# Attention with a block mask, then a gated feed-forward: the first batch loaded by casting transfers, transposed two token tiles at a time, and masked by rows copied on chip

## The chip, the cores and the metric

One core of a Trainium2 chip. The metric is the device time of one execution in microseconds (us), median over several executions.

Engines are named as the profile names them: PE is TensorE (PEld its weight loads), DVE VectorE, ACT ScalarE, POOL GpSimd, SP SyncE. Each engine works through its own instructions in the order in which the program lists them.

## The reference, cut to what matters

```python
# q, k, v: (4 batches, 8 heads, 768 tokens, 64), float32
scores = scale * q @ k.T                    # per batch and head
scores = where(mask, scores, -1e9)          # mask: blocks of 32 x 32 tokens,
                                            # window, first/last block, 3 sampled blocks per row
attn   = softmax(scores)
x      = (attn @ v)                         # as (3072 tokens, 512)
xn     = x / sqrt(mean(x*x) + 1e-6) * rms_g
out    = (silu(xn @ w_gate) * (xn @ w_val)) @ w_out     # 512 -> 1536 -> 512
```

The kernel adds the mask inside the scores matmul: besides the 64 rows of a head, K and Q carry 24 more, one for each block of 32 tokens. K has a 1 in the row of its block, and Q has 0 or -32768 in each row.

## The kernel before: the parts that matter here

Heads are worked in pairs, four to a batch. A unit is a strip of one to three query tiles of 128 tokens, over all eight heads; when the four pairs of a unit have been through attention, its rows can be normalised and go through the feed-forward. Until then PE has no feed-forward work.

```python
KQ = D + NB                                                   # 64 + 24 = 88
UNITS = [(0, 0, 1), (0, 1, 1), (0, 2, 2), (0, 4, 2)]          # (batch, first tile, tiles)
...
# mask columns go into the buffer aug, beside K and Q, before the transposes
nc.vector.tensor_copy(out=aug[0][:, 0, :, :, D:KQ], in_=kmb)
nc.scalar.copy(out=aug[0][:, 1, :, :, D:KQ], in_=qmb)
...
def fill(g, i, eng):              # cast a float32 load to bfloat16, into aug
    copy(eng, aug[g % NAUG][:, i, :, :, 0:D], raws[g][:, i]...)
...
def tp(g, i, n, pool):            # one transpose for each head and token tile, mask columns with it
    ...
        nc.tensor.transpose(
            out=t_[0:KQ, m, :], in_=aug[g % NAUG][:, i, e, c, 0:KQ], identity=ident)
```

Everything after a hand-written start is put in order by a list scheduler at build time. It takes, again and again, the instruction that can start first by its own table of durations, from start times that are also given by hand:

```python
free = {"PE": 5.2, "ACT": 6.0, "DVE": 4.9, "POOL": 4.9, "DMA": 2.1}
...
kk = (int(t1 * 20), o["prio"], o["n"])      # earliest start, then priority
```

The order is fixed when the kernel is built; what differs on the chip only makes engines wait.

The softmax here doesn't subtract the row's maximum and nothing guards it: scores larger than these inputs give would overflow.

## Time and profile before

| | before |
|---|---|
| time, median of the first 3 runs (range) | 313.67 us (313.28 to 314.38) |
| span of the profiled run | 311.3 us |
| first transpose of K | 6.07 us |
| first scores | 8.04 us |
| first gate matmul of the feed-forward | 28.56 us |
| first output matmul | 45.59 us |

The last four rows are starts in the timeline of PE. They mark how far the kernel is: attention can begin, attention runs, the first unit has been through all four pairs, the feed-forward's first product is ready. The page, windows and chain of this kernel are shown in the prediction. Two more views are needed to read what follows. The first is the head of VectorE in the timeline (start, length, engine, line, operation, tiles):

```profile
4.68 0.24 DVE L139 TENSOR_SCALAR Bneg<-Bm 32x32 bf16<-32x32 bf16 x1
...
5.28 0.73 DVE L190 CAST aug<-qkv 128x768 bf16<-128x768 f32 x1
```

The mask is ready by 5 us, and the next work is the cast of the first pair. The second is PE in the same view:

```profile
6.07 0.98 PE L220 MATMUL tp<-ident,aug 128*88 128x128 bf16 x14 [0.80 <-DVE aug L190]
...
8.04 0.50 PE L243 MATMUL s__202<-X 88*128 88x128 bf16 x6
...
28.56 1.06 PE L346 MATMUL gp<-xn,wg 128*128 128x128 bf16 x16
```

### The profile page before, as it was taken

The page shows a single profiled execution, that of the slowest core. Times are in us where ns is not written, and L with a number is a line of the kernel's source. Part 1 is how long each engine was busy: PE and PEld are TensorE (multiplying, and loading weights), DVE is VectorE, ACT ScalarE, POOL GpSimd, SP SyncE. Part 2 cuts the span into 40 slices and gives each one's busy share as a digit, 9 for nine tenths or more (in the row PEclk, how much of TensorE's full clock was granted, in tenths as well). Part 3 has the DMA queues.
Part 4 walks back from the last instruction along what each step waited for, and adds up shares of the span by engine and source line. Part 5 has one row for each costly group of instructions (what it writes and reads, how often), then busy time and mean ns, then how long its engine had stood idle before and what let it go on. Part 6 is the DMA issues. An engine that isn't in the chain of part 4 may idle for free.

```text
span 311.3 us, 7229 instructions
## 1 busy us (share of the span) xinstructions
PE 300.7 (97%) x3015; PEld 201.8 (65%) x3015; DVE 188.0 (60%) x411; ACT 204.1 (66%) x306; POOL 26.3 (8%) x44
## 2 busy tenths in 40 slices
PE   6899999998999999999999999999999999999994
PEld 3888998776777766665666666666656556546541
DVE  6775487756468859646755844754587627517600
ACT  3789888788778778787887877877623333233312
POOL 5594000000001001001000100100010000000000
PEclk9999999999999999999999999999999999999999
DMA  7999996999999999710972300030012020020022
GB/s 222 393 196 203 243 285 137 259 334 220 250 357 254 228 262 273 158 37 2 186 161 45 84 2 35 2 86 6 31 47 40 2 99 3 0 101 2 0 101 101
DMA packets 69187, 42.39 MB, mean 136 GB/s; under 512 B 48036, under 2 KB 65956, under 8 KB 69156
## 3 DMA queue, kind: packets, MB, share of 16 engines
q1 hardware_dynamic: 63328, 37.23, 45.7%
q0 software_dynamic: 5792, 4.72, 9.8%
q8 instruction: 23, 0.38, 0.5%
q14 instruction: 8, 0.07, 0.1%
q10 hardware_dynamic: 36, 0.00, 0.0%
HBM read 28.57 MB, written 6.29 MB: 112 GB/s over the span
## 4 chain that ended last, share of the span: by engine, by line
PE 90%; DMA 5%; ACT 2%; DVE 1%; SPq 0%; issue 0%; POOL 0%; ACTq 0%; DVEq 0%
PE gp L346 20%; PE yp L379 20%; PE vp L346 20%; DMA X<-aug 2%; DMA qkv<-in_k_dram 2%; ACT pt L254 2%; PE tp L220 1%; PE tr L314 0%; SPq L70 0%; PE o__3524 L268 0%; PE o__2246 L268 0%; PE o__2882 L268 0%; PE o__1425 L268 0%; PE o__3944 L268 0%; PE o__3095 L268 0%; PE o__2679 L268 0%
## 5 line engine op out<-in xcount | busy, mean ns | idle before, releaser
L361 DVE SCALAR_TENSOR_TENSOR uu<-th,gp 128x384 bf16<-128x384 bf16 (+1 forms) x90 | 52.1, 580 | 69.0 <-ACT th L355 67.3
L346 PE MATMUL gp<-xn,wg 128*128 128x384 bf16 (+2 forms) x480 | 74.3, 294 | 0.8 <-DVE uu L361 0.8
L346 PE MATMUL vp<-xn,wv 128*128 128x384 bf16 (+2 forms) x480 | 74.3, 294 | 0.0
L379 PE MATMUL yp<-wo,hp 128*128 128x512 bf16 x288 | 69.7, 379 | 0.0
L355 ACT ACTIVATE th<-gp 128x384 bf16<-128x384 f32 (+1 forms) x90 | 46.3, 514 | 33.5 <-PE gp L346 31.5
L346 PEld LDWEIGHTS <-wg 128*128 128x128 bf16 x480 | 43.2, 98 | 22.6 <-issue 1.0
L370 DVE TENSOR_TENSOR hp<-uu,vp 128x384 bf16<-128x384 bf16 (+1 forms) x90 | 50.3, 577 | 12.0 <-PE vp L346 11.2
L346 PEld LDWEIGHTS <-wv 128*128 128x128 bf16 x480 | 43.1, 97 | 21.2
L243 PEld LDWEIGHTS <-X 88*128 88x128 bf16 x480 | 40.8, 97 | 20.1 <-issue 2.2
L379 PEld LDWEIGHTS <-hp 128*128 128x128 bf16 x288 | 28.1, 98 | 28.4
L268 PEld LDWEIGHTS <-pt 128*128 128x128 bf16 x1152 | 41.5, 97 | 5.8 <-ACT pt L254 1.7
L388 ACT ACTIVATE yo<-yp 128x512 f32<-128x512 f32 x23 | 13.8, 598 | 29.9 <-PE yp L379 29.6
L297 POOL TENSOR_TENSOR rs<-ms,nhalf 128x3 f32<-128x3 f32 (+2 forms) x10 | 7.8, 777 | 195.0 <-DVE ms L290 195.0
L190 DVE CAST aug<-qkv 128x768 bf16<-128x768 f32 x28 | 15.3, 560 | 4.8 <-DMA X<-aug 3.6
L304 DVE SCALAR_TENSOR_TENSOR xq<-xo,rs,gB 128x512 bf16<-128x512 f32 x24 | 16.8, 747 | 0.6
L290 DVE CUSTOM_DVE_ANT_0 sc<-xo 128x512 bf16<-128x512 f32 x24 | 16.6, 691 | 0.7
L220 PE MATMUL tp<-ident,aug 128*88 128x128 bf16 x96 | 7.2, 220 | 1.8 <-DVE aug L190 0.8
L190 DVE CAST vaug<-qkv 128x768 bf16<-128x768 f32 x14 | 7.7, 553 | 1.1 <-DMA qkv<-in_v_dram 1.1
L190 DVE COPY X<-tp 88x768 bf16<-88x768 bf16 (+2 forms) x17 | 7.3, 472 | 1.2 <-PE tp L220 1.2
L220 PEld LDWEIGHTS <-aug 128*88 128x88 bf16 x96 | 6.0, 120 | 2.4 <-POOL aug L188 0.9
L88 PE MATMUL zp<-zt 128*128 128x512 bf16 x9 | 3.5, 564 | 1.3 <-DVE zt L85 1.3
L188 POOL CAST aug<-qkv 128x768 bf16<-128x768 f32 x4 | 3.3, 834 | 5.0 <-DMA qkv<-in_k_dram 5.0
(536 smaller groups left out, 352.4 us busy)
## 6 DMA issues: line engine op xcount, KB each, us to landing
qkv<-in_k_dram SPq DMA_DIRECT2D x16, 384.0 KB, 6.9
qkv<-in_q_dram SPq DMA_DIRECT2D x16, 384.0 KB, 6.5
qkv<-in_v_dram SPq DMA_DIRECT2D x16, 384.0 KB, 7.0
out_dram<-yo SPq DMA_DIRECT2D x24, 256.0 KB, 2.0
wg<-in_moe_w_gate_dram POOLq DMA_DIRECT2D x4, 384.0 KB, 7.6
wv<-in_moe_w_val_dram POOLq DMA_DIRECT2D x4, 384.0 KB, 8.7
wo<-in_moe_w_out_dram POOLq DMA_DIRECT2D x2, 768.0 KB, 21.9
gB<-in_moe_rms_g_dram SPq DMA_DIRECT2D x1, 256.0 KB
```

Source lines behind the costliest of these rows:

```text
L190: nc.vector.tensor_copy(out=out, in_=in_)
L220: nc.tensor.transpose(out=t_[0:KQ, m, :], in_=aug[g % NAUG][:, i, e, c, 0:KQ], identity=ident)
L243: nc.tensor.matmul(out=s_[:, e, j * w:(j + 1) * w], lhsT=x[0:KQ, 0, e, jt * P:(jt + 1) * P], rhs=x[0:KQ, 1, e, c0 * P:c0 * P + w], start=T ...
L268: nc.tensor.matmul(out=o_[:, t, e, :], lhsT=pt[:, jt, e, t * P:(t + 1) * P], rhs=va[:, (2 * pr + e) * NC + jt, 0:D + 1], start=(jt == 0), ...
L290: nc.vector.tensor_tensor_reduce(out=sc, in0=x, in1=x, scale=1.0 / DM, scalar=1e-6, op0=ALU.mult, op1=ALU.add, accum_out=mss[u][:, t:t + 1])
L304: nc.vector.scalar_tensor_tensor(out=xqs[u][:, t, :], in0=xos[u][:, t].rearrange("p h d -> p (h d)"), scalar=mss[u][:, t:t + 1], in1=gB, o ...
L346: nc.tensor.matmul(out=p_[:, j, :].rearrange("p (t w) -> p t w", w=P), lhsT=w_[:, c, f_ * P:(f_ + 1) * P], rhs=xns[u][:, :, c, :], start=( ...
L355: nc.scalar.activation(out=t_, in_=tiles["gp", u, f], func=AF.Tanh, scale=0.5)
L361: nc.vector.scalar_tensor_tensor(out=t_, in0=tiles.pop(("th", u, f)), scalar=1.0, in1=tiles.pop(("gp", u, f)), op0=ALU.add, op1=ALU.mult)
L370: nc.vector.tensor_tensor(out=hps[u][:, f * fg:(f + 1) * fg, :], in0=tiles.pop(("uu", u, f)), in1=tiles.pop(("vp", u, f)), op=ALU.mult)
L379: nc.tensor.matmul(out=y_, lhsT=hps[u][:, f, t * P:(t + 1) * P], rhs=wo[:, f, :], start=(f == 0), stop=(f == NF - 1))
L388: nc.scalar.activation(out=o, in_=y_, func=AF.Copy, scale=0.5)
```

## The change

The intent: fewer transposes, and an earlier first unit. A transpose turns two token tiles of 64 columns at once (128 wide) instead of one tile with its mask (88 wide). So the mask rows can't ride along: a small mask is transposed once, completed by two matmuls, and copied on VectorE into the buffers of the other pairs. Pairs 2 and 3 are loaded by DMAs that cast to bfloat16, so they need no cast on an engine. The second half of Q of all pairs is loaded after the first weights. The units of the first batch become 1, 2 and 3 tiles, and small filler matmuls are put where the scheduler foresees that PE waits, to keep its clock up. The core of the diff:

```diff
-    NSLOT, NAUG, NRAW, NWARM = 5, 2, 3, 9
-    UNITS = [(0, 0, 1), (0, 1, 1), (0, 2, 2), (0, 4, 2)]
+    NSLOT, NAUG, NRAW, NWARM = 5, 2, 3, 6
+    UNITS = [(0, 0, 1), (0, 1, 2), (0, 3, 3)]
 ... [cut]
+    for c in range(NC):
+        nc.tensor.transpose(out=kt_[0:KQ, c, :], in_=km8[:, c, :], identity=ident)
+    Kind = const.tile([32, NC, P], BF16, name="Kind")
+    nc.vector.tensor_copy(out=Kind[0:NB], in_=kt_[0:NB])
+    nc.scalar.copy(out=X[0][D:KQ, 0], in_=kt_[D:KQ]...to_broadcast([NB, 2, S]))
+    idle(1500)
 ... [cut: some 17 small mask operations on VectorE, which end with Bneg]
+    for h in range(2):
+        nc.tensor.matmul(out=qt[0:KQ, 0:S // 2], lhsT=Bneg[0:NB, 0:KQ], rhs=Kind[...], ...)
+        copy(("DVE", "ACT")[h], X[0][D:KQ, 1, :, ...], qt[D:KQ, 0:S // 2]...)
+    def mask_k(s_):
+        nc.vector.tensor_copy(out=X[s_][D:KQ, 0], in_=X[0][D:KQ, 0])
+    def mask_q(s_, h):
+        nc.vector.tensor_copy(out=X[s_][D:KQ, 1, :, w_], in_=X[0][D:KQ, 1, :, w_])
 ... [cut: load0, casting DMAs on POOL's queue for pairs 2 and 3]
+    def tp(g, i, lo, hi, pool):
+        for e in range(2):
+            for m, c in enumerate(range(lo, hi, 2)):
+                n = min(2, hi - c) * D
+                nc.tensor.transpose(
+                    out=t_[0:n, e, m, :], in_=R[g][:, i, e, c * D:c * D + n], identity=ident)
 ... [cut]
+        if e == "PE" and t1 < 40.0 and t1 - free["PE"] > 0.25:
+            idle(1000 * (t1 - free["PE"] - 0.1))
```

In `tp` an odd piece of three tiles (`lo` to `hi`) ends in a transpose that is 64 wide.

## The prediction

> **What bounds the kernel now.** I read the page first: engine shares and the slice table, to see which engine is full and where it is not.
>
> ```profile
> PE 300.7 (97%) x3015; PEld 201.8 (65%) x3015; DVE 188.0 (60%) x411; ACT 204.1 (66%) x306; POOL 26.3 (8%) x44
> PE   6899999998999999999999999999999999999994
> PEclk9999999999999999999999999999999999999999
> ```
>
> TensorE is full from the second tenth to the tail, at full clock, so removing work from any other engine after about 30 us buys nothing; only fewer matmul columns, or holes filled, can. To size the holes I add up what the 3015 matmuls need, at spacings taken from the chain in order of time: 56 ns for 128 columns (16 in 0.89 us), 110 for 256 (8 in 0.88), 162 for 384 (4 in 0.65), 216 for 512 (9 in 1.94), 32 for an attention-times-V matmul (12 in 0.38). Gate and value projections: batch 0 10.8 + 21.1, the other six units 93.3, together 125.2 us. Output projection 288 x 0.216 = 62.1. Scores 96 x 0.056 + 96 x 0.110 + 288 x 0.162 = 62.6. Attention times V 1152 x 0.032 = 36.9. Normalised rows' transposes 24 x 0.056 = 1.3; K and Q transposes 96 x 0.056 = 5.4. Sum 293.5 us. The first transpose starts at 6.07 and the last output matmul ends near 307.2, so 301.1 us hold 293.5 of work: **7.6 us of holes**, beside a head of 6.1 and a tail of 4.1.
>
> Next the table of windows, for where they lie (columns: PE, PEld, DVE, ACT, POOL busy with counts, clock, DMA share, GB/s).
>
> ```profile
> 5.00:10.00 5.00, 3.15 (x48) 2.65 (x47) 2.90 (x10) 3.81 (x8) 0.37 (x1) 1.00 0.98 330
> 10.00:15.00 5.00, 4.50 (x85) 4.45 (x86) 4.03 (x11) 3.34 (x5) 3.59 (x6) 1.00 1.08 402
> 15.00:20.00 5.00, 4.94 (x92) 4.60 (x90) 4.48 (x15) 4.32 (x6) 5.00 (x7) 1.00 1.20 213
> 20.00:25.00 5.00, 4.14 (x75) 3.57 (x73) 2.78 (x11) 4.49 (x7) 4.12 (x7) 1.00 1.31 200
> 30.00:35.00 5.00, 5.00 (x93) 4.86 (x91) 2.26 (x6) 4.21 (x7) 0.00 (x0) 1.00 1.27 212
> ```
>
> The reader is to see that the holes are before 30 us, while VectorE is near full from 10 to 20 and ScalarE from 15 on. Until the first gate matmul at 28.56 PE issues 96 K/Q transposes (5.4), 96 scores of 128 columns (5.4), 24 of 256 (2.6), attention times V 3.8, one transposed unit 0.2: 17.4 us in 22.5. **5.1 of the 7.6 us lie there.** The chain, then, for what holds them open:
>
> ```profile
> 2.34 7.24 DMA qkv<-in_k_dram
> 9.63 0.83 POOL aug L188
> 10.51 1.04 PE tp L220 x14
> ...
> 21.32 0.82 ACT pt L254
> 22.19 0.46 PE o__534 L268 x9
> ...
> 23.02 0.82 ACT pt L254
> ```
>
> First a load (pair 1's K lands at 9.6), a cast on POOL and transposes; then exponentials, each followed by V matmuls. PE has no feed-forward work to fill with, because that needs unit 0 of all four pairs. The last pair's transposes run at 17.1, its V matmuls end at 22.65 and the gate starts at 28.56. Weights are not the cause: the first two pieces are issued at 13.6 and 14.7 and take 6.5 and 7.3 us, so they are in at 22.0. Two later waits matter less:
>
> ```profile
> PE gp L346 <- DVE uu L361: 0.8, 1, 0.8
> DVE aug L190 <- DMA X<-aug: 3.6, 3, 1.9
> ```
>
> VectorE, stuck in order behind a cast that waits for a DMA transpose, costs PE 0.8 us at 76.
>
> **What the Trainium skill says.** "TensorE: Matmul & The Clock Gate", section Back-to-back issue gap: a warm matmul of N columns takes N/2.4 + 2.5 ns, 55.8 for 128; the trace gives 56, so a transpose costs its 128 columns however many rows it turns, and two 64-wide token tiles in one transpose halve the count. "VectorE: DVE Perf Modes", section Side-by-side: a copy inside SBUF may pass two fp32 or four bf16 elements a cycle and one that reads PSUM cannot use both ports. The casts agree (768 fp32 in 0.56 us); so do the evictions (768 bf16 from PSUM in 0.55), and they will not get cheaper by using 64 instead of 88 partitions. No copy of the mask's kind is in this trace; from the page's 693 ns for 2048 elements I estimate 0.56 us for 1536 and 0.36 for 768. "DMA: Bandwidth & Descriptors", section Issuing engines are not separate DMA queues: all queues share 16 engines. The trace agrees: the first loads land about 1.0 us apart (8.6, 9.6, then three more by 12.6, five more by 17.4), near 393 KB a microsecond. "SBUF — State Buffer", section SBUF: two separate sides: two-port VectorE copies keep GpSimd from writing descriptors. Weakly supported here: one DMA instruction on POOL took 1.11 us beside VectorE casts, most others 0.74 to 0.77.
>
> **The change, part by part.** *Transposes.* Pair 0 needs 14 (three for each head's K, four for Q's pieces), the others 14 each: 56 for 96, so PE loses 40 x 56 ns = 2.2 us. A fourth unit is now transposed on PE and units are of 1, 2, 3, 3 tiles instead of 1, 1, 2, 2, so 36 row transposes for 24: +0.7. Six small mask matmuls at 24 us: +0.2. Net work on PE, which is what counts after 30 us, **-1.3 us**.
>
> *Loads.* The first four pairs need 12 loads of 393 KB now. After it, the second half of Q, four half-loads, goes behind the first weights, and 10 loads' worth precede them. K of pair 3 is about the eighth instead of the tenth, and is transposed as it lands, with no cast on POOL: about 13.4 us, where its transposes now run at 17.1. Casting on the way saves VectorE and POOL the four fills of pairs 2 and 3 (4 x 0.56 to 0.83 us), but takes POOL's issue time, ten instructions of 0.75 before the fourth weight piece.
>
> *VectorE, 5.3 us to the first gate matmul.* Fills of pairs 0 and 1: 0.55 + 0.91. Evictions for pair 0, half on ScalarE: 1.0; for three pairs K twice 0.56 and Q twice 0.32, 1.76 x 3 = 5.3. Mask rows: 3 x 0.56 and 3 x 0.36 = 2.8, all new. V: 1.8. The normalising of unit 0 and some of unit 1: 0.46 x 6 = 2.8, sum of squares and scale 1.5. Mask evict 0.35. Sum 17.0, so no gate matmul before about 22.3 if all of it goes first; some can be put off. By the other chain: K of pair 3 at 13.4, transposes and eviction 1.5, scores and two exponentials in turn 2, V 0.5, then normalise 0.46, square 0.77, power 0.58, scale 0.74, transpose 0.38, evict 0.58 = 3.5, with waits between about 4.5: 21.9. I take **22 us for the first gate matmul, not 28.6.**
>
> *Holes until 22 us.* ScalarE makes one 768-column exponential in 0.71 us (two in 1.52 at most); PE needs 0.34 + 6 x 0.032 = 0.53 us for it. From 8.0 to 22 ScalarE, less about 1.5 us of evictions, makes some 17: 9.0 us of PE, plus some 48 transposes 2.7, plus 0.2: 11.9 in 16 us. That is 4.1 of holes if nothing is better packed. If the three 1024-column exponentials of the two-tile unit come in early and no load is late, it is nearer 2. I take 3.1 for 5.1, **-2.0 us**. After that PE has feed-forward work and is full.
>
> *Head.* Masks no longer go through the fill, and the first K comes by halves to two engines, but a longer string of small mask operations runs on VectorE first. **-0.2.** *Later.* The schedule now counts on longer DMA transposes and the weights are in some 5 us earlier; I give half of the 0.8 and the 2.5 us of other holes a little: **-0.5**. Sum 1.3 + 2.0 + 0.2 + 0.5 = 4.0: 313.67 - 4.0 = **309.7 us**.
>
> **The rivals.** *VectorE takes the bound.* For: 17 us of work in the 17 us after 5.3, and POOL, busy with issuing, can't help. Against: the Q second halves and half the mask rows wait. Then the gate starts at 25 or later, the holes stay at 5, and only 2 us are gained: 311.5. *Loads come late.* For: DMA share is over 1 from 10 us, two queues share the engines, and casting DMAs may cost more or wait for descriptors. Against: the weight phase, all casting, reads 12.7 MB from 15 to 46 us, 410 GB/s. If pair 3 comes 3 us later, as much of the start is lost: 312. *Batch 1 is not ready earlier.* PE would reach it 3 us sooner, and the 0.8 hole at 76 us grows: gain 1.5 to 2.5. *Everything packs.* Holes at the start 1.5, head 0.5 shorter, no later wait: 1.3 + 3.6 + 0.5 + 1.2 = 6.6, 307.1.
>
> **Range and chances.** The 1.3 us of matmul work are nearly certain; the rest is the packing of the start, from -0.5 to +5.3. That gives 307.1 to 313; with a little beyond each end cut for the 8 in 10, 306.9 to 312.6. Two per cent is 307.4 us, so only the case where everything packs passes it: 0.18. Slower by 2% would need a new wait of 10 us: 0.02.
>
> **What would show it.** Right if transposes of K and Q number 56, the first gate matmul is near 22 us, VectorE is over nine tenths busy from 8 to 20 us, and TensorE has no hole after 30 us larger than 1 us. Wrong at the load step if K of pair 3 lands after 15; at the VectorE step if it is below eight tenths there; at the sum if the gate starts early and the end does not move, for then the holes went further down. Filler matmuls make PE look busy at the start, so matmuls are to be counted there, not busy time.

## The result, and the profile after

| | before | after | predicted |
|---|---|---|---|
| time, median of 4 runs (range) | 314.02 us (313.28 to 314.60) | **322.39 us** (321.77 to 322.48) | 309.7 (306.9 to 312.6) |
| ratio, 95% interval | 1 | 1.0264 (1.0236 to 1.0291) | |
| span of the profiled run | 311.3 | 320.3 | |
| first transpose of K | 6.07 | 9.89 | about 5.9 |
| first scores | 8.04 | 12.54 | |
| first gate matmul | 28.56 | 32.26 | 22 |
| first output matmul | 45.59 | 56.36 | |

The kernel became 2.6% slower, and the prediction was wrong in the sign. Here and below, a ratio is the mean time of one kernel's fast runs over that of the kernel before in the same rounds, so it is not quite the ratio of the medians quoted beside it. Executions over 1.5% slower than the fastest of the same kernel are left out of the means.

First the page of the kernel after: engine shares, and PE and its clock in 40 slices of the span.

```profile
PE 309.5 (97%) x2952; PEld 203.7 (64%) x2981; DVE 195.9 (61%) x438; ACT 207.3 (65%) x313; POOL 26.5 (8%) x43
...
PE   6899999999999999999999999999999999999995
...
PEclk9599999999999999999999999999999999999999
```

PE looks as full as before, but busy is not useful: 139 of its matmuls up to 60 us are warm-up or fillers (before: 9). And its second slice, from 8 to 16 us, ran near half clock; the records have half clock from 9.19 to 16.01 us, 6.8 us long. The table of windows, with the same columns as in the prediction:

```profile
5.00:10.00 5.00, 2.79 (x36) 2.17 (x33) 4.05 (x23) 2.52 (x3) 2.13 (x3) 0.92 1.16 268
10.00:15.00 5.00, 5.00 (x46) 4.50 (x46) 4.40 (x11) 2.37 (x4) 4.25 (x6) 0.50 1.24 253
15.00:20.00 5.00, 5.00 (x57) 3.85 (x56) 3.88 (x10) 2.33 (x3) 3.21 (x5) 0.90 1.31 203
20.00:25.00 5.00, 4.74 (x79) 4.27 (x77) 4.18 (x13) 4.73 (x7) 0.00 (x0) 1.00 1.43 197
30.00:35.00 5.00, 5.00 (x89) 4.38 (x86) 2.42 (x8) 4.57 (x6) 1.73 (x3) 1.00 1.05 148
```

The column to read is ScalarE's, because it makes the exponentials that attention waits for: 2.52, 2.37 and 2.33 us of 5 from 5 to 20 us, where it had 3.81, 3.34 and 4.32. The first exponential starts at 13.42 us instead of 8.57. Over the first 30 us, in the same columns, before and then after:

```profile
0.00:30.00 30.00, 24.92 (x377) 20.57 (x378) 20.29 (x65) 21.89 (x29) 19.72 (x36) 1.00 1.07 255
```

```profile
0.00:30.00 30.00, 25.33 (x311) 21.81 (x312) 20.85 (x70) 17.87 (x22) 15.18 (x29) 0.89 1.11 200
```

PE's busy time is the same, but ScalarE did 4.0 us less. The chain that ended last shows what held the start (start, length, engine, tile, line):

```profile
4.75 0.55 DVE Kind L146
...
7.54 0.18 DVE Bneg L181
...
7.76 0.37 PE qt L185
8.15 0.95 DVE XA L103
...
9.28 0.57 DVE aug L103
...
9.89 1.22 PE tp L283 x8
```

Where the chain before began with a load, this one goes through VectorE. What it waited for is in the list of waits up to 60 us (us in total, times, longest):

```profile
ACT pt L317 <- PE s__736 L302: 2.6, 1, 2.6
...
DVE Kind L146 <- PE kt__135 L144: 2.5, 1, 2.5
```

VectorE stood 2.5 us before the copy `Kind`, which needs the transposed mask; that stands on PE behind 24 warm-up matmuls, which start 100 ns apart (fillers of the same shape at full clock: 52 to 53). No run took these out, so what they cost here isn't known. The small mask operations don't depend on `Kind`, but they follow it in order, and so do the casts: the first half of pair 0's K is cast at 9.28 us, though it was issued at 0.81 and landed 2.5 us later. The other wait is after the first gate group. PE there:

```profile
32.26 0.83 PE L412 MATMUL gp<-xn,wg 128*128 128x128 bf16 x12
...
34.13 1.40 PE L283 MATMUL tp<-ident,aug 128*128 128x128 bf16 x8
...
40.66 0.83 PE L412 MATMUL gp<-xn,wg 128*128 128x128 bf16 x12
```

The second gate group comes 8.4 us after the first (before: 4.1 us, 28.56 to 32.65). Between them stand the transposes of the second halves of Q, fillers and attention.

Last, where along the run the loss lies. I worked it out by counting the matmul time that is still to be done at a moment, from the exponentials, feed-forward products and outputs that are not yet finished, and taking it from the time that is left until PE ends. What remains is time that PE will lose from then on. (Work done ahead makes the figure a little low or negative, so only the differences count.)

| at us | 20 | 30 | 45 | 60 |
|---|---|---|---|---|
| before, us still to be lost | 5.9 | 1.6 | -0.6 | 0.5 |
| after | 11.4 | 8.0 | 1.3 | 0.5 |
| after minus before | 5.5 | 6.4 | 1.9 | 0.0 |

PE ended at 307.2 and at 316.4 us, 9.2 apart. So 9.2 - 5.5 = 3.7 us had been lost by 20 us, and some 7 of the 9.2 by 45; none of the loss came after 60. The largest part, 6.4 - 1.9 = 4.5 us, lies between 30 and 45 us, after the first gate matmuls: from start to start in the trace, PE spent 2.7 us of that stretch on 16 transposes of second halves of Q and 1.4 on 22 fillers, where the kernel before had neither (its transposes of Q were done by 20 us).

### The profile page after: what moved, and what is told of

Its sections match the earlier page's. It is cut to its first block, busy times and chain, and to the rows that moved or that the text cites. A ratio compares the mean times of both kernels' runs of the same rounds, so it can differ in the third digit from the quotient of the medians.

```text
span 320.3 us, 7154 instructions
## 1 busy us (share of the span) xinstructions
PE 309.5 (97%) x2952; PEld 203.7 (64%) x2981; DVE 195.9 (61%) x438; ACT 207.3 (65%) x313; POOL 26.5 (8%) x43
## 4 chain that ended last, share of the span: by engine, by line
PE 94%; DVE 3%; issue 1%; ACT 1%; ACTq 0%
PE gp L412 20%; PE vp L412 20%; PE yp L445 19%; PE ob L331 11%; PE ob L117 3%; PE tp L283 2%; PE tr L380 1%; DVE xo L343 1%; ACT pt L317 0%; DVE XA L103 0%; DVE rz L342 0%; DVE XA L196 0%; PE s__284 L302 0%; PE kt__135 L144 0%; PE s__259 L302 0%
## 5 line engine op out<-in xcount | busy, mean ns | idle before, releaser
L445 PE MATMUL yp<-wo,hp 128*128 128x512 bf16 x259 | 64.9, 379 | 1.5
L412 PEld LDWEIGHTS <-wg 128*128 128x128 bf16 x432 | 40.2, 97 | 23.6 <-issue 0.2
L302 PEld LDWEIGHTS <-XA 88*128 88x128 bf16 x432 | 38.5, 99 | 22.4 <-issue 2.1
L331 PE MATMUL ob<-vaug,pt 128*128 128x65 bf16 x1152 | 42.5, 193 | 0.0
L343 DVE TENSOR_TENSOR xo<-ob,rz 128x384 f32<-128x384 f32 (+2 forms) x36 | 18.5, 513 | 1.2
L353 DVE CUSTOM_DVE_ANT_0 sc<-xo 128x512 bf16<-128x512 f32 x24 | 16.6, 690 | 0.7
L117 PE MATMUL ob<-zt 128*128 128x120 bf16 x139 | 13.4, 252 | 2.3 <-DVE zt L110 1.5
L342 DVE RECIPROCAL rz<-ob 128x6 f32<-128x6 f32 (+2 forms) x36 | 6.8, 190 | 12.9 <-PE ob L331 12.3
L103 DVE CAST aug<-qkv 128x768 bf16<-128x768 f32 (+2 forms) x27 | 13.8, 534 | 0.2 <-issue 0.2
L117 PEld LDWEIGHTS <-zt 128*128 128x128 bf16 x139 | 11.1, 118 | 4.2 <-issue 1.9
L103 DVE COPY XA<-tp 64x256 bf16<-64x256 bf16 (+2 forms) x25 | 9.7, 393 | 1.8 <-PE tp L283 1.3
```

The costliest lines, as they stand in the source:

```text
L103: nc.vector.tensor_copy(out=out, in_=in_)
L117: nc.tensor.matmul(out=zp[:, 0:n], lhsT=zt[:, 0:P], rhs=zt[:, 0:n], start=True, stop=True)
L302: nc.tensor.matmul(out=s_[:, e, j * w:(j + 1) * w], lhsT=x[0:KQ, 0, e, jt * P:(jt + 1) * P], rhs=x[0:KQ, 1, e, c0 * P:c0 * P + w], start=T ...
L331: nc.tensor.matmul(out=o_[:, t, e, :], lhsT=pt[:, jt, e, t * P:(t + 1) * P], rhs=va[:, (2 * pr + e) * NC + jt, 0:D + 1], start=(jt == 0), ...
L343: nc.vector.tensor_tensor(out=xos[u][:, :, 2 * pr:2 * pr + 2, :], in0=o_[:, :, :, 0:D], in1=rz.unsqueeze(3).to_broadcast([P, nt, 2, D]), o ...
L353: nc.vector.tensor_tensor_reduce(out=sc, in0=x, in1=x, scale=1.0 / DM, scalar=1e-6, op0=ALU.mult, op1=ALU.add, accum_out=mss[u][:, t:t + 1])
```

## The experiments

All are edits of the kernel after, timed over 3 rounds or more against the kernel before (its medians: 313.23 us beside e1 to e4, 313.76 beside e5 to e8, 314.13 beside e9 to e11, 313.71 beside e12 to e15, 313.8 beside e16). Since these differ by up to 0.9 us, and the kernel after was timed beside 314.02, I give differences between calls by the medians and, where it matters, by the ratios too. All are correct, except the last. My theory was a chain of three at the start: VectorE's order delays the first transpose, the waiting PE loses its clock, and mask copies crowd VectorE. Rivals were the fillers in PE's way, weights issued late, the new cut of the units, and, once I had seen the spacing of the new transposes, their mixed widths.

### e2_mask_first: the order of VectorE alone

```diff
-    nc.vector.tensor_copy(out=Kind[0:NB], in_=kt_[0:NB])
-    nc.scalar.copy(out=X[0][D:KQ, 0], ...)            # K mask rows
     ... [small mask operations, ending with Bneg]
+    nc.vector.tensor_copy(out=Kind[0:NB], in_=kt_[0:NB])
+    nc.scalar.copy(out=X[0][D:KQ, 0], ...)
```

> The changed kernel with the two copies of the transposed mask moved behind the small mask operations on VectorE, so that these run in the 2.5 us in which VectorE now waits. Theory L: the mask matmuls start near 5.4 instead of 7.8 us, the first K transpose near 7.5 instead of 9.9, the clock does not fall or falls for less, and the time drops by 2.4 us plus up to 3.4 us of half-clock: 316.5 to 320. Theory F or W alone: within 1 us of 322.4.

Measured 320.23 us, ratio 1.0214 (1.0167 to 1.0262). VectorE in the timeline:

```profile
4.53 0.30 DVE L177 TENSOR_SCALAR Bneg<-tf 32x32 bf16<-32x32 f32 x1
4.75 0.55 DVE L179 COPY Kind<-kt__135 24x768 bf16<-24x768 bf16 x1
```

The small operations now lie in the wait: `Bneg` starts at 4.53 instead of 7.54. The first transpose moves from 9.89 to 9.08, scores from 12.54 to 11.47, the gate from 32.26 to 30.34, and the time falls by 2.2 us by the medians, by (1.0264 - 1.0214) x 314 = 1.6 us by the ratios. So the order was a cause. It wasn't all of the head's delay: the mask matmul starts only at 6.94, for it stands behind the fillers of `idle(1500)`, and the casts still follow its evictions.

### e3_warm and e1_no_fill: the clock

```diff
-    idle(1500)
+    idle(2600)                          # e3
     ... [the two mask matmuls]
+    idle(1200)                          # e3
 ...
-        if e == "PE" and t1 < 40.0 and t1 - free["PE"] > 0.25:      # e1
-            idle(1000 * (t1 - free["PE"] - 0.1))                    # e1
```

> The changed kernel with more filler matmuls before and after the mask matmuls, so that TensorE is never idle for over 1 us before the first K transpose; nothing real is moved. If the 6.8 us at half clock (9.2 to 16.0 us) cost what their matmuls lack: clock full from 6 us on, 2 to 3.4 us faster, 319 to 320.4. If the start is bound by VectorE and ScalarE in those microseconds anyway: under 1 us faster, though the clock is full.

> The changed kernel without the filler matmuls that its schedule puts into TensorE's stream (about 87 of its 139; the warm-up and the 28 before the mask matmuls stay). Theory L (the start is late because the mask chain on VectorE waits for the mask transpose, and the clock then drops): fillers only fill waits, so at most 1.5 us faster, 321 to 322.5, and the clock may stay low longer. Theory F (fillers stand in the way: they take PE time when real work is ready, and some wait for the VectorE read of the bank that they write): 3 to 5 us faster, 317.5 to 319.5. Theory W (late weights): no change.

e3: 321.66 us, ratio 1.0263 (1.0224 to 1.0303). e1: 324.21 us, 1.0344 (1.0302 to 1.0386). In e3 the window from 10 to 15 us, which had a granted clock of 0.50, is at full clock:

```profile
10.00:15.00 5.00, 4.07 (x60) 3.28 (x58) 4.78 (x12) 2.16 (x5) 4.58 (x7) 1.00 1.22 234
```

Yet only 0.7 us come of it by the medians, and nothing by the ratios. The test is not clean, because the added fillers also delay the first scores, to 13.40 from 12.54 us: from there to the gate it is 18.7 us, where it was 19.7. About 1 us is therefore what I would give the clock in the kernel after, as an estimate. Without the fillers (e1) the clock stays at half for 20.5 us instead of 6.8, and 1.8 us more are lost (2.5 by the ratios). The single executions of one kernel bear on the clock too. The kernel after took 321.77 us at a granted clock of 0.995, and 322.39 to 322.48 at 0.988 or 0.989; e5 took 318.29 and 318.68 at 0.999, and 320.08 and 320.25 at 0.993. So one and the same program is 0.6 to 1.8 us longer with more time at half clock, and a median mixes such executions. The fillers earn their place in this kernel; the half clock looks like a symptom of the waiting more than its cause.

### e4_no_gate: weights issued late

```diff
-    [prev] + {(3, 0): [("rsq", 0)], (4, 0): [("rsq", 1)]}.get((i, m), [])
+    [prev]
```

> The changed kernel without the two waits that hold the fourth gate and value weight piece and the output weights behind the normalising of units 0 and 1. Theory W (late weights starve TensorE until 56 us): output matmuls start near 46 instead of 56 us and the time drops by 2 to 4 us. Theories L and F: under 1 us, since TensorE has other work from 32 us on, or slower, as the weights crowd the loads of the second halves of Q.

321.94 us, ratio 1.0276 (1.0236 to 1.0316): no change. In the kernel after the first weights of the output projection are issued at 40.67 us, late beside the plan, but nothing that matters waits for them. This rival falls.

### e5_mask_dma, e6_fill_early, e7_fill_early_mask_dma: mask copies and the first casts

All on top of e2. e5 copies the mask rows by DMA instead of on VectorE; e6 casts pair 0 before the mask's evictions, two pieces on each engine; e7 does both.

```diff
 def mask_k(s_):                                                     # e5, e7; mask_q alike
-    nc.vector.tensor_copy(out=X[s_][D:KQ, 0], in_=X[0][D:KQ, 0])
+    nc.sync.dma_start(out=X[s_][D:KQ, 0], in_=X[0][D:KQ, 0])
 ...
     ... [Bneg]                                                      # e6, e7
+    copy("ACT", R[0][:, 0, 1:2, 0:2 * HD], A[0][:, 0, 1:2, 0:2 * HD])
+    copy("ACT", R[0][:, 1, :, 0:D], A[0][:, 1, :, 0:D])
     nc.vector.tensor_copy(out=Kind[0:NB], in_=kt_[0:NB])
+    copy("DVE", R[0][:, 0, 0:1, 0:2 * HD], A[0][:, 0, 0:1, 0:2 * HD])
+    copy("DVE", R[0][:, 1, :, D:HD], A[0][:, 1, :, D:HD])
```

> The kernel with the mask copies moved behind the small mask operations (e2, 320.2 us), and the nine copies of mask rows to the X buffers of pairs 1 to 3 by DMA instead of VectorE, in the same places of the order: some 4.5 us less on VectorE between 11 and 26 us. Theory V (VectorE, with evictions and mask copies, holds the start until 25 us): 2 to 4 us faster than e2, 316 to 318. If the order of the work and not VectorE's load holds it: within 1 us of 320.2. If the 2 us of a DMA come on the path: slower.

> e2 with the casts of pair 0's first K and Q before the mask matmuls' evictions, on VectorE and ScalarE, as the data lands from 3.3 us on. Theory L: the first K transpose moves from 9.1 to about 7.4 us and the end with it: 1 to 2 us faster than e2, 318 to 319.2. If what follows is bound elsewhere: the first transpose earlier, the end within 0.7 us of 320.2.

> Both. Theories L and V together: the gains add, 3 to 6 us faster than e2, 314 to 317. If one wait hides the other: no better than the better of the two alone.

| | us | ratio (95%) | first scores | first gate |
|---|---|---|---|---|
| e2 | 320.23 | 1.0214 (1.0167 to 1.0262) | 11.47 | 30.34 |
| e5 | 319.38 | 1.0168 (1.0129 to 1.0207) | 10.65 | 28.60 |
| e6 | 319.97 | 1.0180 (1.0147 to 1.0213) | 9.69 | 28.37 |
| e7 | 318.48 | 1.0142 (1.0109 to 1.0176) | 9.89 | 27.84 |

The scores and gates are those of the profiled execution, which is one of the two fastest of its kernel in e5 (318.68) and the fastest in e6 (318.74). The casts alone bring the scores 1.8 us earlier and save only 0.3 us by the medians, 1.1 by the ratios. The windows from 10 to 15 us say why, of e6 and then of e7:

```profile
10.00:15.00 5.00, 4.99 (x64) 3.92 (x62) 4.81 (x11) 3.54 (x4) 4.51 (x6) 1.00 1.22 238
```

```profile
10.00:15.00 5.00, 4.99 (x65) 3.96 (x61) 3.90 (x9) 3.54 (x4) 4.25 (x7) 1.00 1.25 248
```

In e6 VectorE is busy 4.81 of 5 us, and with the mask copies off it, 3.90. With full clock in both, e7 against e6 is the cleanest measure of these copies: 1.5 us by the medians, 1.2 by the ratios. Some of them are also longer while POOL is at work. In the kernel after, on VectorE and on POOL:

```profile
11.47 0.97 DVE L192 COPY XA<-XA 24x1536 bf16<-24x1536 bf16 x1
```

```profile
11.20 0.83 POOL L101 CAST vaug<-qkv 128x768 bf16<-128x768 f32 x1
```

The same copy takes 0.55 us at 19.81, where POOL does nothing. (It isn't so for all: a half-size copy at 17.54, beside an issue of POOL, took 0.35 like those alone. No run tested the cause.) Together the two edits save 1.75 us on top of e2, 2.3 by the ratios.

### e9_wide, e10_group, e11_wide_early_dma: the widths of the transposes

The count of transposes came out as planned (groups of PE by shape, up to 60 us: count, then busy us and mean ns of one):

```profile
L283 PE MATMUL tp<-ident,aug 128*128 128x128 bf16 x20 | 3.5, 286 | 1.2 <-DVE aug L103 1.2
L283 PE MATMUL tp<-ident,qkv 128*128 128x128 bf16 x20 | 2.8, 222 | 0.0
L283 PE MATMUL tp<-ident,qkv 128*64 128x128 bf16 x8 | 1.9, 243 | 0.0
L283 PE MATMUL tp<-ident,aug 128*64 128x128 bf16 x8 | 1.9, 260 | 0.0
```

That is 40 of 128 and 16 of 64, together 56. But in the pieces of three tiles they alternate in width, and there the trace has starts at 17.849 (128 wide), 17.996 (64), 18.172 (128), 18.332 (64), 18.507 (128): 147 to 176 ns apart, at full clock, instead of 56. Being narrower than 128 is not by itself the reason, nor is any change of width: the 88-wide transposes of the kernel before start 55 to 56 ns apart, and so do an 88-wide one and a 128-wide score beside it (56 ns, at 13.77 and 14.44 us). A piece is four transposes; two pieces take 1.33 us, from 17.85 to the next matmul at 19.18, and with equal widths they take 0.44 (e9 below). Seven pieces are of this kind (four for the second half of Q, three for the first), so PE loses 7 x (1.33 - 0.44) / 2 = 3.1 us.

e9 turns tiles (0, 1) and (1, 2) of a piece, all 128 wide, the middle tile twice. e10 keeps the shapes but groups them. e11 is e7 with e9's transposes, that is, all repairs together.

```diff
-            for m, c in enumerate(range(lo, hi, 2)):
+            for m, c in enumerate((lo, lo + 1) if hi - lo == 3 else range(lo, hi, 2)):   # e9, e11
 ...
-        for e in range(2):
-            for m, c in enumerate(range(lo, hi, 2)):
+        for m, c, e in [(m, c, e) for m, c in enumerate(range(lo, hi, 2)) for e in range(2)]:   # e10
```

(In e9 and e11 the evictions take the tiles from where they now lie.)

> The changed kernel with every transpose of a three-tile piece 128 columns of weights wide: tiles 0,1 and 1,2 instead of 0,1 and 2 alone. The number of transposes, evictions and their sizes stays. Theory T (in the trace a 64-wide weight load between 128-wide ones makes the spacing 147 to 176 ns instead of 56; in seven pieces of four transposes each that is 0.44 us each): 2.6 to 3.3 us faster, 319 to 319.8, the pieces taking 0.22 instead of 0.66 us. If TensorE waits there for evictions anyway: under 1 us.

> The changed kernel with the same four transposes of a piece in another order: first the two 128-wide, then the two 64-wide. If the change of width costs: two changes a piece instead of four, half of theory T's loss comes back, 1.3 to 1.7 us faster, 320.7 to 321.1. If a 64-wide load is slow in itself: no change.

> All repairs that helped, together: mask copies behind the small mask operations, casts of pair 0 before the mask evictions, mask rows by DMA (318.5 us so far), and 128-wide transposes. If the losses are separate: 3 us off, 315 to 316, still above the kernel before. If one hides another: 316.5 to 318.5.

e9: 320.49 us, ratio 1.0203 (1.0134 to 1.0272), spacing 55 to 56 ns. e10: 321.31 us, 1.0226 (1.0167 to 1.0286), with spacings of 55, 148, 80 and 151 ns: the 150 stand at each change between 128 and 64. e9's gain of 1.9 us holds some of the clock too, which happened to be full from 5.18 us in its profiled execution (319.05 us). Its two executions at a granted clock of 0.989 took 320.86 and 321.01, 1.5 us less than the kernel after at 0.988 or 0.989. The cleanest pair is e7 and e11, both at full clock in every window from 5 us on. The same eight transposes, of e7 and then of e11:

```profile
13.71 1.40 PE L287 MATMUL tp<-ident,qkv 128*128 128x128 bf16 x8
```

```profile
13.21 0.61 PE L287 MATMUL tp<-ident,qkv 128*128 128x128 bf16 x8
```

e11 takes 316.68 us, ratio 1.0076 (1.0020 to 1.0132), 1.8 us less than e7 (2.1 by the ratios). So of the 3.1 us that the changes of width take on PE about 2 reach the end; the rest lay beside waits.

### e8_units, e12_replan, e13_replan_units: the order

e8 is the kernel after with the units of before. e12 is e11 with the scheduler's start times set to those measured (PE 7.3, VectorE 8.5, ScalarE 8.0 us) and the moved copies and casts taken off its VectorE. e13 is e12 with the units of before, and two settings that fitted them.

```diff
-    UNITS = [(0, 0, 1), (0, 1, 2), (0, 3, 3)]                              # e8, e13
+    UNITS = [(0, 0, 1), (0, 1, 1), (0, 2, 2), (0, 4, 2)]
 ...
-    free = {"PE": 5.2, "ACT": 5.3, "DVE": 4.9, "POOL": 3.3, "DMA": 2.1}    # e12, e13
+    free = {"PE": 7.3, "ACT": 8.0, "DVE": 8.5, "POOL": 3.3, "DMA": 2.1, "SPQ": 6.0}
 ...
-    NPT, NXN, NHP, NPET = 3, 3, 2, 4                                       # e13
+    NPT, NXN, NHP, NPET = 3, 3, 2, 3
-    AHEAD, HURRY = 0.4, ("av", "xo", "sq", "rsq", "xq", "tr", "cp")        # e13
+    AHEAD, HURRY = 0.0, ("av", "xo", "sq", "rsq", "xq", "tr", "cp")
```

> The changed kernel as it was, with the first batch cut into units of 1, 1, 2, 2 token tiles as before, not 1, 2, 3. Theory U (the second unit's longer exponentials come between those of unit 0, so its feed-forward work comes late, and the third unit waits for all second halves of Q): 2 to 4 us faster, 318 to 320.5, with the gate matmuls of unit 0 done before 40 us. Otherwise within 1 us of 322.4.

> The repaired kernel (e11, 316.7 us), its order laid anew with the times at which its engines were measured to be free (TensorE 7.3, VectorE 8.5, ScalarE 8.0 us) and the mask rows and first casts taken off VectorE in the plan. If the rest of the loss (3 us above the kernel before) is an order laid for a start 2 to 4 us too early: 1 to 3 us faster than e11, 313.5 to 315.5. If the order of this plan is no better (the plan itself ends later than the one before): within 1 us of 316.7.

> As e12, with units of 1, 1, 2, 2 tiles again, three units' rows transposed on TensorE instead of four, and no look-ahead for unit 0; of some 80 settings the one that the kernel's own plan gives the earliest end. If the loss that is left comes from the 1, 2, 3 cut (feed-forward work stalls at 28 to 36 us behind the second halves of Q): 311.5 to 314, level with the kernel before or up to 2 us faster. If the cut does not matter once the rest is mended: 315 to 317.

e8: 326.18 us, ratio 1.0385 (1.0356 to 1.0414). e12: 321.93 us, 1.0257 (1.0208 to 1.0306). e13: 316.94 us, 1.0098 (1.0054 to 1.0143). The cut of the units is not the culprit in the kernel after: the old one costs 3.8 us more in e8. With the new plan it is the other way round: e13, with the old units and two settings chosen for them, is 5.0 us faster than e12. So what the cut is worth depends on the plan, and neither run gives it alone. And a plan with truer numbers is not a better plan: e12 loses 5.3 us against e11, most of it by the plan (its one execution at a granted clock of 0.999 took 321.03). This limits what all single edits here can tell: an effect of 1 us is within what a different order can give or take.

### e14_e11_no_fill and e15_replan_units_no_fill: fillers again

Both take the in-schedule fillers out, of e11 and of e13.

```diff
-        if e == "PE" and t1 < 40.0 and t1 - free["PE"] > 0.25:
-            idle(1000 * (t1 - free["PE"] - 0.1))
```

> e11 without the fillers that the schedule places; its clock is full from 5.6 us on, so that this time the clock should not drop for long. Theory F (fillers stand in the way: two to nine of 52 ns at a time, and five of them wait for a VectorE read of their bank): 0.7 to 2 us faster, 314.7 to 316. If they only fill waits: within 0.5 us. If the clock drops again: slower, and the records show it.

> e13 without the fillers of the schedule. Same alternatives: 0.7 to 2 us faster than e13 if fillers stand in the way, equal if not, slower if the clock drops.

316.62 us, ratio 1.0081 (1.0036 to 1.0126), and 317.40 us, 1.0113 (1.0074 to 1.0153): the same as e11 and e13 within their spread. The clock was at half for 3.4 us in e14, and for 10.2 in e15 (e13: 6.8). So taking the fillers out gained nothing that these runs can show, and in these two kernels they aren't needed either.

### e16_no_q_mask: does the mask still hold e11's head?

Wrong on purpose (relative error 0.56): e11 without the two mask matmuls of Q and their evictions; the rows are zeroed by early DMAs.

```diff
-    for h in range(2):
-        ... [qt matmul and its copy into X[0][D:KQ, 1]]
+    for j_ in range(3):            # early, on ScalarE's queue
+        nc.scalar.dma_start(out=xq0[:, 512 * j_:512 * (j_ + 1)], in_=zt[D:KQ, :])
```

> Wrong on purpose: e11 without the two matmuls of the query mask and their two evictions into pair 0's X buffer; these rows are zeroed by an early DMA instead, so that nothing is masked, and copied on as before. Theory M (mask rows that no longer ride along in the transposes of K and Q are a serial step of their own ahead of the first scores, and this is what e11 still loses): first transpose near 6, first scores near 8.3 instead of 9.8 us, 1 to 2 us faster than e11, 314.7 to 315.7. If the start is not what e11 loses: within 0.5 us of 316.7.

318.11 us, ratio 1.0123 (1.0071 to 1.0176): not faster than e11 but 1.4 us slower. The first transpose stays at 7.43 us (7.39 in e11), the first scores come at 9.14 instead of 9.84, but pair 1's Q is cast and transposed later (from 12.61 instead of 11.83), its scores start at 16.31 instead of 14.15 us, after a wait of 1.70 for the DMA that copies mask rows, and the clock was at half from 16.6 to 20.0. The edit disturbed what it wasn't meant to, so it doesn't decide.

### What stays open

From the kernel after to e11, 322.39 - 316.68 = 5.7 us are accounted for (by the ratios 5.9): the order on VectorE 2.2, first casts and mask copies together 1.75, widths 1.8. The clock's part is inside these, since it came back with them. e11 is still 2.5 us over the kernel before (ratio 1.0076), though its gate starts earlier (27.65 against 28.56 us). The timeline of PE in e11:

```profile
27.65 0.83 PE L420 MATMUL gp<-xn,wg 128*128 128x128 bf16 x12
...
34.70 0.83 PE L420 MATMUL gp<-xn,wg 128*128 128x128 bf16 x12
```

The second gate group comes 7.1 us later, and until then PE has attention, the second halves of Q and fillers. By the same count as above, e11 still has 3.2 us more to lose than the kernel before at 30 us and 1.7 more at 45. Its PE ends 3.2 us later (310.4 against 307.2), so by this count all of its loss lies after 30 us, and the later scores (9.84 against 8.04 us) had cost nothing by then. It isn't the fillers: without them (e14) PE was busy for only 4.00 of 5 us from 30 to 35. In that window of e11 VectorE is nearly full:

```profile
30.00:35.00 5.00, 4.83 (x76) 3.86 (x74) 4.76 (x15) 3.64 (x6) 2.20 (x4) 1.00 1.20 203
```

Before, it had 2.26 there (last line of the prediction's windows). The order after the gate, and the evictions and normalising that now meet on VectorE, are what is left as a cause, but that is argued, not shown: no run changes them alone. No version ran faster than the kernel before.

## Why the prediction was wrong

**The step that failed is "Head. ... -0.2".** It saw that "a longer string of small mask operations runs on VectorE first", and still counted a gain. Measured, the first transpose comes 3.8 us later (9.89 against 6.07) and the first scores 4.5 us. It named the operations, but gave no number for them and didn't see their place: they stand on an in-order engine behind a copy that waits 2.5 us for PE, and the first cast stands behind them all. e2 and e7 moved things in that order and got 2.2 and, with the mask copies, another 1.75 us.

**"Holes until 22 us", -2.0, fell with it.** It counted on 17 exponentials from 8.0 us on. The first started at 13.42, ScalarE was half empty until 20 us, and the gate came at 32.26, not 22. It also set gain equal to an earlier gate. e7 and e11 show the mistake: their gates at 27.84 and 27.65 us are earlier than before's, and both kernels end later than it; in e11 the second group follows only after 7.1 us. Nor was PE full from then on, as the prediction had it ("After that PE has feed-forward work and is full"): 4.5 of the 9.2 us were lost between 30 and 45 us. The prediction's last paragraph named the sign of an early gate without gain ("if the gate starts early and the end does not move"), but gave it no chance of its own.

**"Net work on PE", -1.3, had the wrong sign.** The count of 56 transposes was right. The spacing of 56 ns came from 88-wide transposes beside 88 and 128; 28 of the 56 alternate between 128 and 64 and cost 3.1 us more on PE. The section that the prediction cites gives its formula for a single matmul, and says that in a stream of weight loads and matmuls both set the spacing, some 81 ns at 128 columns. The 81 isn't seen here (55 to 56 where widths are equal), but the warning held. So the 2.2 us saved became 0.9 lost, before the 0.9 that the sum had for extra row transposes and mask matmuls.

**Right.** *Loads*: K of pair 3 landed at 13.7 us, where 13.4 was predicted; casting DMAs did their part, and loads coming late was no rival. (One reading against that rival doesn't stand: the weight phase was not "all casting", since six plain loads of 393 KB were issued between 30.8 and 36.4 us.) *Copies*: the estimates of 0.56 and 0.36 us were good for copies alone (0.55 and 0.35), and short for three of those beside POOL (0.97, 0.76 and 0.72). *After 60 us*: nothing gained and nothing lost, so the "later" term of -0.5 was empty as well.

**Half right.** *VectorE takes the bound* was named as a rival at 311.5 us. It shows once the head is mended: in e6 VectorE was busy 4.81 of 5 us from 10 to 15. In the kernel after it was at 4.40 and 3.88 from 10 to 20, under the nine tenths I had asked for, since the late head left it less to do there.

**The chances.** "Slower by 2% would need a new wait of 10 us: 0.02" treated terms as one sum around a gain. The expected gain of 4.0 needed the head on time; each term was counted from a start that the change itself moved. With head, widths and copies against it, 322.39 - 314.02 = 8.4 us were lost, and up to 60 us no wait of VectorE, ScalarE or PE was longer than 2.6.

## What to carry to other kernels

Before counting what a change saves later, write down the first instructions of each in-order engine in their new order, with what each waits for: independent small work behind one early wait delays everything that follows, and can be moved ahead of the wait. Look at the spacing of neighbouring matmuls on PE: here it went from 56 to some 150 ns where weights of 128 and of 64 columns alternated, and doing some work twice to keep one width was cheaper. Where a static order is made from a table of durations, a single edit moves the whole order; compare pairs that differ in one thing at the same clock, and don't read effects of a microsecond from others.

## What the Trainium skill lacked or had wrong

- "TensorE: Matmul & The Clock Gate", section Weight-path perf modes — Fast Weight Load (FWL) and DoubleRow, says that the fast load is on when the number of weights is 128 and the type is not FP32. It doesn't say what a change of width costs between back-to-back matmuls. "TensorEngine Tiling (Array Packing)", section Key Properties, says that a change of tiling mode drains TensorE, and the page lists 128x64 as a mode of its own, but gives no time; no view here shows in which mode a transpose ran. Here transposes that alternate between 128 and 64 wide start 147 to 176 ns apart at full clock; grouped, 55 ns (128 after 128), 148 (to 64), 80 (64 after 64) and 151 (back to 128). And 88-wide weights start 55 to 56 ns apart, one after another and beside 128-wide ones, so that the missing fast load alone doesn't show in the spacing.
- "SBUF — State Buffer", section Who interferes with whom, has the exclusive lock between VectorE's two-port copies and GpSimd. The runs agree in direction (a 24x1536 copy took 0.55 us alone, 0.97 and 0.76 us while POOL was at work), but the page gives no figure for a cast on POOL beside such a copy.
- No page that I used tells what filler matmuls are worth: taken out, they cost 1.8 us where PE waited long (half clock for 20.5 us instead of 6.8), and nothing clear of the spread in e14 and e15 (3.4 and 10.2 us at half clock).
